# Moving the decoding of float64 weights behind the softplus of the step in front of it, and the split of a gathered tile by one group

## The chip, the cores and the metric

The kernel runs on one core of a Trainium2 chip. The metric is device time in microseconds (us) of one execution; lower is better. Times are of the whole program: attention, a dense softplus layer and a mixture of experts, fused into one launch.

## The reference, cut to what matters

```python
def reference(q, k, v, moe_w_in, moe_w_out, moe2_w_skip, moe2_w_gate, moe2_w1, moe2_w2):
    attn = softmax(rotate(q) @ rotate(k).T / 8) @ v                # 2 x 8 heads x 576 tokens x 64
    x = attn.transpose(0, 2, 1, 3).reshape(1152, 512)
    h = x @ w_in                                                   # 512 x 2048, float64
    x = softplus(h) @ w_out                                        # 2048 x 512, float64
    # softplus: max(h, 0) + log1p(exp(-|h|))
    # then: tokens with x @ w_skip > 0 go to the best of 8 experts (x @ w_gate);
    # out = x + probability * (relu(x @ w1[e]) @ w2[e]); the other tokens keep x
```

The two weight matrices of the middle layer come as float64 and are read by the kernel as 64-bit integers; it turns them into float32 itself.

## The kernel before, in words

Matrix products are made in two parts for accuracy: each operand is split into a rounded high part and the rest (`gh`/`gl`, `xh`/`xl`, two layers of `w`), and three products of the parts are added in PSUM.

The middle layer works in steps. A step (phase, f) takes group f of 128 of the 2048 hidden columns and one chunk of tokens. There are four phases (`ranges`): phase 0 takes tokens 0 to 511 with groups 0 to 5, phase 1 takes tokens 512 to 1151 with all groups 0 to 15, phases 2 and 3 take tokens 0 to 255 and 256 to 511 with groups 6 to 15. In a step, `hidden` issues the products h on TensorE (L581; two halves a and b of 320 tokens in phase 1, one piece of 512 in phase 0), then the softplus: Abs, Relu, Exp, 1+y and Ln on ScalarE (L596, L598, L600, L603, L606), three VectorE instructions (L605, L608, L610), the rounding `gh` on ScalarE (L612) and the rest `gl` on VectorE (L613). `second` multiplies gh and gl with the output weights into acc (L622); it is traced two steps behind `hidden`.

The weights of a group are loaded and decoded once, in `weights`: two halves (w_in and w_out), each of which is one DMA of 512 KB into `raw` (two buffers), three integer instructions on VectorE that put the sign, exponent and mantissa bits together (L563, L564, L565), the rounding on ScalarE (L567) and the rest on VectorE (L568). All decoded groups then stay in SBUF. Groups 0 and 1 are decoded during attention; the table `ahead` says before which step of which phase each other group is decoded: entry (z, fw) of phase p decodes group fw in front of step (p, z).

Each engine works through its own queue in order. Within what the data allow, a scheduler at build time merges the traced instructions into these queues; `issue_after(ins)` makes the instructions of its block that are on the engine of `ins` stand behind `ins` in that queue. It adds no wait between engines.

Near the end of phase 3, `moe2.gather` transposes the first gathered tile of the expert layer and splits it into two parts (L873 on ScalarE and VectorE, named `split`). `XGT` names the step behind which this is traced, and `hidden` of all later steps is put behind `split` by `issue_after`. After the last step a part with a hand-written TensorE order follows: the last groups' products (`rest`), with products mh of the expert layer (L1197) in between.

Of the kernel before, what the change touches and what calls it, by code (L numbers as in the profile page):

```python
# [9 lines left out]
F32 = mybir.dt.float32  # L10
# [31 lines left out]
EARLY = ((2, 11), (3, 9), (3, 10), (3, 11), (3, 12))  # L42

N0 = 6
XGT = (3, 13)
REST = ((12, 13), (14,))


# [487 lines left out]
class Moe1:  # L536
# [34 lines left out]
    def hidden(self, ci, f, hp, tp, gq):  # L571
        nc, w = self.nc, self.w[f]
        c0, n, _ = self.CH[ci]
        nb = 2 if n > 512 else 1
        m = n // nb
        ps = [hp.tile([128, 512], F32, name=f"h{ci}{f}{c}", tag="h") for c in range(nb)]
        z = 0
        for k in range(4):
            for x, src in ((0, self.xh), (0, self.xl), (1, self.xh)):
                for c in range(nb):  # L580
                    nc.tensor.matmul(  # L581
                        ps[c][:, 0:m], lhsT=w[:, 0, x, 128 * k : 128 * k + 128],
                        rhs=src[:, k, c0 + m * c : c0 + m * c + m], start=z == 0, stop=z == 11,
                    )
                z += 1
        def t(nm, dt=F32, bufs=2):
            x = (gq if bufs == 4 else tp).tile([128, 640], dt, name=f"{nm}{ci}{f}", tag=nm, bufs=bufs)
            return x

        y, r, u, gh, gl = t("y"), t("r"), t("u"), t("gh", F32R, 4), t("gl", F32R, 4)  # L590

        ln = u[:, 320 : 320 + n] if n <= 320 else u[:, 0:n]
        y, r, u, gh, gl = (x[:, 0:n] for x in (y, r, u, gh, gl))
        cs = [(ps[c][:, 0:m], slice(m * c, m * c + m)) for c in range(nb)]
        for hv, c in cs:
            nc.scalar.activation(y[:, c], hv, AF.Abs)  # L596
        for hv, c in cs:
            nc.scalar.activation(r[:, c], hv, AF.Relu)  # L598
        for hv, c in cs:
            nc.scalar.activation(y[:, c], y[:, c], AF.Exp, scale=-1.0)  # L600

        for hv, c in cs:
            nc.scalar.activation(u[:, c], y[:, c], AF.Copy, bias=1.0)  # L603
        for hv, c in cs:
            nc.vector.scalar_tensor_tensor(y[:, c], u[:, c], 1.0, y[:, c], op0=ALU.subtract, op1=ALU.subtract)  # L605
            nc.scalar.activation(ln[:, c], u[:, c], AF.Ln)  # L606
        for hv, c in cs:
            nc.vector.tensor_sub(r[:, c], r[:, c], y[:, c])  # L608
        for hv, c in cs:
            nc.vector.tensor_add(r[:, c], r[:, c], ln[:, c])  # L610
        for hv, c in cs:
            nc.scalar.copy(gh[:, c], r[:, c])  # L612
            nc.vector.tensor_sub(gl[:, c], r[:, c], gh[:, c].bitcast(F32))  # L613
        return gh, gl

    def out_mm(self, ci, f, g, acc, f0, f1, only=None):
# [453 lines left out]
def attention_moe_moe_kernel(ctx: ExitStack, tc, q, k, v, w_in, w_out, w_skip, w_gate, w1, w2, tab, out):  # L1070
    nc = tc.nc

    def pool(stack, name, bufs=1, space=None, **kw):
        if space is not None:
            kw["space"] = space
        return stack.enter_context(tc.tile_pool(name=name, bufs=bufs, **kw))
# [10 lines left out]
    with ExitStack() as s1:  # L1087
# [4 lines left out]
        moe1 = Moe1(nc, w_in, w_out, xh, xl)  # L1092
# [25 lines left out]
        with ExitStack() as s2:  # L1118
            gq, gp = pool(s2, "gq"), pool(s2, "gp")
            ring = [(pool(s2, "wb0"), 3), (pool(s2, "wb1"), 2), (wc, 4), (wa, 2)]  # L1120
            tp = pool(s2, "tp")
            hp, accp = pool(s2, "hp", 2, PSUM), pool(s2, "accp", 5, PSUM)
            psa = pool(s2, "psa", 1, PSUM)

            part = tp.tile([128, 4, 512], F32, name="part")
            ranges = ((0, 0, N0), (1, 0, 16), (2, N0, 16), (3, N0, 16))
            steps = [(ph, ci, f) for ph, (ci, f0, f1) in enumerate(ranges) for f in range(f0, f1)]
            due, pend, accs = [], [], {}
            ahead = {0: [(0, 2), (1, 3), (2, 4), (3, 5), (5, 6)],
                     1: [(0, 7), (2, 8), (3, 9), (5, 10), (6, 11), (8, 12), (9, 13), (11, 14), (12, 15)], 2: [], 3: []}  # L1130

            def ready(ph, t):
                if ph == 0:
                    nc.scalar.copy(part[:, t, :], accs[ph][t])
                    return
                x2 = tp.tile([128, 512], F32, name=f"x2{t}", tag="x2", bufs=4)
                if ph == 1:
                    nc.scalar.copy(x2, accs[ph][t])
                else:
                    nc.vector.tensor_add(x2, accs[ph][t], part[:, t, :])  # L1140
                k = 128 * ORDER2.index(t)
                nc.sync.dma_start(x2d[k : k + 128, 0:DM], x2)
                for r, ap in out_rows(out, t):
                    nc.sync.dma_start(ap, x2[r])
                due.append((t, x2))

            def second(group):

                ph, ci = group[0][:2]
                _, f0, f1 = ranges[ph]  # L1150
                ts = Moe1.CH[ci][2]
                if group[0][2] == f0:
                    accs[ph] = {t: accp.tile([128, 512], F32, name=f"acc{ph}{t}", tag="acc") for t in ts}
                last = group[-1][2] == f1 - 1
                for t in ts:
                    for _, _, f, g in group:
                        moe1.out_mm(ci, f, g, accs[ph], f0, f1 - 1, t)
                    if last:
                        ready(ph, t)

            for ph, ci, f in steps:
                for z, fw in ahead[ph]:
                    if z == f:
                        wb, n = ring[(0, 0, 0, 1, 1, 2, 2, 2, 2, 0, 0, 0, 1, 3)[fw - 2]]

                        with ExitStack() as order:
                            for done in att.parted[-2:] if fw >= LATE_W else ():
                                order.enter_context(tc.issue_after(done))
                            moe1.weights(fw, wb, st, n)
                with ExitStack() as order:  # L1170
                    if (ph, f) > XGT:
                        for done in moe2.split:
                            order.enter_context(tc.issue_after(done))
                    pend.append((ph, ci, f, moe1.hidden(ci, f, hp, gp, gq)))
                if len(pend) > 2 and (ph, f) not in HOLD:
                    second([pend.pop(0)])
                if due and (ph, f) >= (2, 10):
                    t, x2 = due.pop(0)
                    moe2.logits(t, moe2.turned(t, x2, hp, tp), psa)
                    if not due:  # L1180
                        moe2.route(*((4, 5) if ph == 2 else (0, 2)), psa)
                if (ph, f) == (2, 15):
                    moe2.first_tile(psa)
                    moe2.fetch(0, sp)
                if (ph, f) in EARLY:
                    c = EARLY.index((ph, f))
                    raw = st.tile([128, 1024], F32, name=f"wr{c}", tag="st", bufs=2)
                    moe2.load_chunk(raw, 0, c)
                    moe2.early.append(moe2.split_w(0, c, raw))
                if (ph, f) == XGT:  # L1190
                    st0 = moe2.gather(0, gq, accp, "acc")
            mh0 = [accp.tile([128, 512], F32, name=f"mh0{c}", tag="acc") for c in range(2)]
            fill = list(moe2.hidden_mm(0, st0, mh0))

            def more(n):
                while n and fill:
                    fill.pop(0)()  # L1197
                    n -= 1

            def rest(t, fs):  # L1200
                for ph, ci, f, g in pend:
                    if f in fs:
                        moe1.out_mm(ci, f, g, accs[ph], N0, 15, t)

            with tc.manual_schedule(engines={nc.tensor.engine}):
                for fs in REST:
                    rest(2, fs)
                    rest(3, fs)
                    more(MORE[4])
                for t in (2, 3):  # L1210
                    rest(t, (15,))
                    ready(3, t)
                more(MORE[0])
                xt = [moe2.turned(t, x2, hp, tp) for t, x2 in due]
                more(MORE[1])
                for (t, _), x in zip(due, xt):
                    moe2.logits(t, x, accp, "acc")
                more(MORE[2])
                moe2.route(2, 2, psa, more)
                more(24)  # L1220
            st0 = moe2.relu(0, st0, sp, mh0)
# [44 lines left out]
```

## Time and profile before

| what | before |
|---|---|
| median of 3 runs | 543.67 us (542.75 to 544.87) |
| the profiled execution | 541.82 us |
| its span of instructions | 540.0 us, so 1.82 us lie around it |
| TensorE (PE) busy | 500.6 us, 93% |
| VectorE (DVE) busy | 437.7 us, 81% |
| ScalarE (ACT) busy | 388.1 us, 72% |
| GpSimd (POOL) busy | 195.8 us, 36%, most of it in attention |
| bytes moved | 67.18 MB, mean 124 GB/s |

Busy shares are means over stages with different limits: attention (about 0 to 210 us), the middle layer (about 183 to 410 us), the experts (about 404 to 540 us). A stage is read by the windows of the trace and by what TensorE waits for in it. PE is the matmul, PEld the load of its stationary operand, which overlaps.

### The profile page before, as it was taken

What the parts mean: (1) busy time and instruction counts of PE and PEld (TensorE: products, weight loads), DVE (VectorE), ACT (ScalarE), POOL (GpSimd) and SP (SyncE); (2) the same over time, 40 slices, a digit from 0 to 9 for tenths busy, and PEclk for the clock granted to TensorE, in tenths of its full rate; (3) what the DMA queues carried; (4) which work ended last, traced back from release to release, by engine and by line L of the source; (5) the groups of instructions that cost most, each with busy time, mean ns of one, the idle gap of its engine ahead of it and who ended that gap; (6) DMA issues with size and microseconds to landing.
All of it is one profiled execution on the core that took longest, in us unless ns stands there. A gap on an engine that the chain in (4) does not pass through costs nothing. (4 is left out here: it accounts for less than half of the span.)

```text
span 540.0 us, 9141 instructions
## 1 busy us (share of the span) xinstructions
PE 500.6 (93%) x2924; PEld 423.8 (78%) x2924; DVE 437.7 (81%) x866; ACT 388.1 (72%) x887; POOL 195.8 (36%) x236
## 2 busy tenths in 40 slices
PE   7899988979988999889999999999998899899994
PEld 3787877857767888779999998999986678677773
DVE  6687876898899999899999944546775789788994
ACT  2588887868877785697676956866783588677881
POOL 2878999979864311000000000001200524522331
PEclk9699999999999999989999999999999999999998
DMA  8797365344354023443433300410325704695300
GB/s 202 189 232 207 81 157 133 100 98 131 94 148 136 2 78 102 139 130 114 142 118 101 134 0 1 157 39 5 126 76 183 286 20 157 215 386 185 117 21 34
DMA packets 43014, 67.18 MB, mean 124 GB/s; under 512 B 9824, under 2 KB 24416, under 8 KB 42960
## 3 DMA queue, kind: packets, MB, share of 16 engines
q1 hardware_dynamic: 39184, 59.60, 37.2%
q0 software_dynamic: 1440, 4.20, 2.1%
q10 hardware_dynamic: 2336, 2.74, 1.6%
q8 instruction: 25, 0.41, 0.3%
q14 instruction: 29, 0.24, 0.2%
HBM read 67.30 MB, written 7.15 MB: 138 GB/s over the span
## 5 line engine op out<-in xcount | busy, mean ns | idle before, releaser
L581 PE MATMUL h<-xh,w 128*128 128x320 f32 (+2 forms) x464 | 105.4, 310 | 0.2 <-ACT P L264 0.2
L622 PE MATMUL acc<-w,gh 128*128 128x512 f32 x288 | 85.0, 401 | 6.1 <-ACT gh L612 6.0
L850 DVE TENSOR_TENSOR ws<-raw,ws 128x1024 fp32r<-128x1024 f32 x67 | 78.8, 1219 | 5.5 <-ACT ws L846 5.3
L581 PEld LDWEIGHTS h<-xh,w 128*128 128x128 f32 x464 | 77.8, 188 | 4.2 <-ACT P L264 0.4
L581 PE MATMUL h<-xl,w 128*128 128x320 f32 (+2 forms) x232 | 69.6, 308 | 0.0
L686 POOL TENSOR_SCALAR sc<-lg 128x2 f32<-128x2 f32 (+1 forms) x3 | 1.0, 327 | 186.5 <-DVE lg L669 186.5
L622 PEld LDWEIGHTS acc<-w,gh 128*128 128x128 f32 x288 | 53.4, 192 | 16.9 <-ACT gh L612 6.8
L846 ACT CAST ws<-raw 128x1024 fp32r<-128x1024 f32 x67 | 66.4, 1062 | 0.2 <-ACT ex L737 0.2
L926 PE MATMUL y<-ws,hT 128*128 128x512 f32 x216 | 57.4, 404 | 1.1 <-DVE ws L850 0.5
L938 POOL DMA_INDIRECT out_dram<-yo,si x9 | 31.5, 3499 | 69.5 <-DVE yo L937 59.2
L264 ACT ACTIVATE P<-s,m 128x576 f32<-128x576 f32 x64 | 48.0, 752 | 10.9 <-DVE m L251 10.5
L251 DVE TENSOR_REDUCE m<-s 128x1 f32<-128x576 f32 x64 | 47.8, 749 | 7.9 <-PE s L243 6.9
L334 PE MATMUL t<-ct,P 128*128 128x128 f32 x288 | 46.2, 283 | 8.1 <-DVE pt L329 3.7
L412 PE MATMUL pv<-pt,vv 128*128 128x320 f32 (+1 forms) x272 | 49.7, 314 | 2.8 <-DVE x L424 2.1
L878 PE MATMUL mh<-ws,xgT 128*128 128x512 f32 x192 | 49.0, 399 | 1.7 <-DVE ws L850 1.3
L622 PE MATMUL acc<-w,gl 128*128 128x512 f32 x144 | 49.3, 392 | 0.0
L596 ACT ACTIVATE y<-h 128x320 f32<-128x320 f32 (+2 forms) x58 | 25.3, 438 | 31.0 <-PE h L581 30.2
L926 PEld LDWEIGHTS y<-ws,hT 128*128 128x128 f32 x216 | 39.0, 188 | 10.8 <-DVE ws L850 1.8
L605 DVE SCALAR_TENSOR_TENSOR y<-u,y 128x320 f32<-128x320 f32 (+2 forms) x58 | 27.3, 484 | 23.0 <-ACT u L603 23.0
L334 PEld LDWEIGHTS t<-ct,P 128*128 128x128 f32 x288 | 34.3, 143 | 14.6 <-DVE pt L329 5.1
L412 PEld LDWEIGHTS pv<-pt,vv 128*128 128x128 f32 x272 | 40.2, 194 | 6.1 <-DVE x L424 3.3
L581 PEld LDWEIGHTS h<-xl,w 128*128 128x128 f32 x232 | 43.3, 188 | 2.1
(266 smaller groups left out, 1122.2 us busy)
## 6 DMA issues: line engine op xcount, KB each, us to landing
raw<-in_moe_w_dram SPq DMA_DIRECT2D x68, 512.0 KB
raw<-in_moe_w_in_dram SPq DMA_DIRECT2D x16, 512.0 KB
raw<-in_moe_w_out_dram SPq DMA_DIRECT2D x16, 512.0 KB
ks<-kT SPq DMA_DIRECT2D x32, 144.0 KB
kl<-kT SPq DMA_DIRECT2D x32, 144.0 KB
qs<-qT SPq DMA_DIRECT2D x32, 128.0 KB
wr<-in_moe_w_dram SPq DMA_DIRECT2D x5, 512.0 KB
x2d<-x SPq DMA_DIRECT2D x9, 256.0 KB
```

The source lines that it names most:

```text
L251: self.latest = nc.vector.tensor_reduce(st["m"][:, a : a + 1], st["ps"][a][:, :, 0:288], axis=AX.XY, op=ALU.max, negate=True)
L264: nc.scalar.activation(P[:, 576 * a : 576 * a + 576].rearrange("p (c n) -> p c n", c=2), ps[:, :, 0:288], AF.Exp, bias=m[:, a : a + 1], ac ...
L334: nc.tensor.transpose(ps[:, 128 * i : 128 * i + 128], src, ident)
L412: nc.tensor.matmul(ps[:, 0:n], lhsT=vv[:, j, :], rhs=pt[:, x, self.place(c, i), 0:n], **se)
L581: nc.tensor.matmul(ps[c][:, 0:m], lhsT=w[:, 0, x, 128 * k : 128 * k + 128], rhs=src[:, k, c0 + m * c : c0 + m * c + m], start=z == 0, stop ...
L605: nc.vector.scalar_tensor_tensor(y[:, c], u[:, c], 1.0, y[:, c], op0=ALU.subtract, op1=ALU.subtract)
L622: nc.tensor.matmul(acc[t], lhsT=g[x][:, 128 * j : 128 * j + 128], rhs=w[:, 1, y, :], start=f == f0 and z == 0, stop=f == f1 and z == 2,)
L846: hi = nc.scalar.copy(w[:, 0], raw)
L850: self.did[T, c] = hi.ins, nc.vector.tensor_sub(w[:, 1], raw, w[:, 0].bitcast(F32)).ins
L878: i = mm()
L926: nc.tensor.matmul(py, lhsT=ht[:, x, o : o + 128], rhs=w[:, y, 512 * j : 512 * j + 512], start=c == 0 and j == 0 and z == 0, stop=c == 3 a ...
L938: nc.gpsimd.indirect_dma_start(out=self.out, out_offset=bass.IndirectOffsetOnAxis(ap=si.bitcast(U32), axis=0), in_=yo, in_offset=None, bou ...
```

## The change

Group 6 is no longer decoded in phase 0; the ten groups 6 to 15 are decoded in phase 1, most of them one step later than before. Their VectorE instructions are put behind `plus`, the last L613 that was traced before them, which is that of the step in front. And `XGT` moves from step (3, 13) to (3, 14).

```diff
-XGT = (3, 13)
+XGT = (3, 14)
...
         for hv, c in cs:
             nc.scalar.copy(gh[:, c], r[:, c])
-            nc.vector.tensor_sub(gl[:, c], r[:, c], gh[:, c].bitcast(F32))
+            self.plus = nc.vector.tensor_sub(gl[:, c], r[:, c], gh[:, c].bitcast(F32))
...
-            ahead = {0: [(0, 2), (1, 3), (2, 4), (3, 5), (5, 6)],
-                     1: [(0, 7), (2, 8), (3, 9), (5, 10), (6, 11), (8, 12), (9, 13), (11, 14), (12, 15)], 2: [], 3: []}
+            ahead = {0: [(0, 2), (1, 3), (2, 4), (3, 5)],
+                     1: [(0, 6), (1, 7), (3, 8), (4, 9), (6, 10), (7, 11), (8, 12), (10, 13), (11, 14), (12, 15)],
+                     2: [], 3: []}
...
                             for done in att.parted[-2:] if fw >= LATE_W else ():
                                 order.enter_context(tc.issue_after(done))
+
+                            if fw >= N0:
+                                order.enter_context(tc.issue_after(moe1.plus.ins))
                             moe1.weights(fw, wb, st, n)
```

No instruction is added or taken away. What the scheduler makes of it is seen at two places.

VectorE where phase 0 ends. Numbers in names are buffers: gl_2983 is of step (0, 4); u_3038 before and u_3021 after are of step (0, 5); u_3108 and u_3091 of step (1, 0); raw_3007 and raw_3015 before, and raw_3047 and raw_3055 after, are the two halves of group 6; raw_3064 is the first half of group 7. Before:

```order
L563 TENSOR_SCALAR wt_3009<-raw_3007 128x512
L564 SCALAR_TENSOR_TENSOR wt_3009<-raw_3007,wt_3009 128x512
L563 TENSOR_SCALAR wt_3017<-raw_3015 128x512
L613 TENSOR_TENSOR gl_2983<-r_2980,gh_2982 128x512
L565 SCALAR_TENSOR_TENSOR wt_3009<-raw_3007,wt_3009 128x512
L564 SCALAR_TENSOR_TENSOR wt_3017<-raw_3015,wt_3017 128x512
L565 SCALAR_TENSOR_TENSOR wt_3017<-raw_3015,wt_3017 128x512
L568 TENSOR_TENSOR w_3006<-wt_3009,w_3006 128x512
L563 TENSOR_SCALAR wt_3066<-raw_3064 128x512
L568 TENSOR_TENSOR w_3006<-wt_3017,w_3006 128x512
L564 SCALAR_TENSOR_TENSOR wt_3066<-raw_3064,wt_3066 128x512
L605 SCALAR_TENSOR_TENSOR y_3036<-u_3038,y_3036 128x512
```

In the change:

```order
L613 TENSOR_TENSOR gl_2983<-r_2980,gh_2982 128x512
L605 SCALAR_TENSOR_TENSOR y_3019<-u_3021,y_3019 128x512
L605 SCALAR_TENSOR_TENSOR y_3089<-u_3091,y_3089 128x320
L608 TENSOR_TENSOR r_3020<-r_3020,y_3019 128x512
L608 TENSOR_TENSOR r_3090<-r_3090,y_3089 128x320
L610 TENSOR_TENSOR r_3020<-r_3020,u_3021 128x512
L610 TENSOR_TENSOR r_3090<-r_3090,u_3091 128x320
L613 TENSOR_TENSOR gl_3023<-r_3020,gh_3022 128x512
L563 TENSOR_SCALAR wt_3049<-raw_3047 128x512
L563 TENSOR_SCALAR wt_3057<-raw_3055 128x512
L605 SCALAR_TENSOR_TENSOR y_3089<-u_3091,y_3089 128x320
```

The softplus of (0, 5) now has no decoding in front of it or in between; group 6 follows it.

VectorE near the end of phase 3. u_5153 is of step (3, 13); u_5196 before and u_5187 after are of (3, 14); u_5230 of (3, 15); xgT is the split. Before:

```order
L613 TENSOR_TENSOR gl_5155<-r_5152,gh_5154 128x256
L873 TENSOR_TENSOR xgT_5178<-xgt_5172,xgT_5177 128x512
L605 SCALAR_TENSOR_TENSOR y_5194<-u_5196,y_5194 128x256
L605 SCALAR_TENSOR_TENSOR y_5228<-u_5230,y_5228 128x256
L608 TENSOR_TENSOR r_5195<-r_5195,y_5194 128x256
L608 TENSOR_TENSOR r_5229<-r_5229,y_5228 128x256
L610 TENSOR_TENSOR r_5195<-r_5195,u_5196 128x256
L610 TENSOR_TENSOR r_5229<-r_5229,u_5230 128x256
L613 TENSOR_TENSOR gl_5198<-r_5195,gh_5197 128x256
L613 TENSOR_TENSOR gl_5232<-r_5229,gh_5231 128x256
```

In the change:

```order
L605 SCALAR_TENSOR_TENSOR y_5185<-u_5187,y_5185 128x256
L608 TENSOR_TENSOR r_5152<-r_5152,y_5151 128x256
L608 TENSOR_TENSOR r_5186<-r_5186,y_5185 128x256
L610 TENSOR_TENSOR r_5152<-r_5152,u_5153 128x256
L610 TENSOR_TENSOR r_5186<-r_5186,u_5187 128x256
L613 TENSOR_TENSOR gl_5155<-r_5152,gh_5154 128x256
L613 TENSOR_TENSOR gl_5189<-r_5186,gh_5188 128x256
L873 TENSOR_TENSOR xgT_5212<-xgt_5206,xgT_5211 128x512
L605 SCALAR_TENSOR_TENSOR y_5228<-u_5230,y_5228 128x256
L608 TENSOR_TENSOR r_5229<-r_5229,y_5228 128x256
```

Step (3, 14) has moved from behind the split to in front of it, beside (3, 13); ScalarE's order moves in the same way.

## Rows read from the trace of the kernel before

**Rows 1.** The page, part 1: busy us (share of the span) and instructions of each engine.

```profile
PE 500.6 (93%) x2924; PEld 423.8 (78%) x2924; DVE 437.7 (81%) x866; ACT 388.1 (72%) x887; POOL 195.8 (36%) x236
```

**Rows 2.** Waits of PE from 190 to 425 us: total, times, longest.

```profile
PE acc L622 <- ACT gh L612: 6.0, 2, 4.0
```

**Rows 3.** Windows: length; busy us of PE, PEld, DVE, ACT, POOL; granted clock; DMA share; GB/s.

```profile
227.20:231.20 4.00, 0.00 (x0) 0.00 (x0) 4.00 (x9) 3.31 (x9) 0.00 (x0) 1.00 0.42 133
231.20:240.00 8.80, 8.79 (x40) 7.72 (x41) 8.80 (x20) 7.59 (x19) 0.00 (x0) 0.81 0.25 80
250.00:260.00 10.00, 10.00 (x62) 9.39 (x61) 9.85 (x23) 5.94 (x16) 0.00 (x0) 1.00 0.41 116
400.00:410.00 10.00, 8.02 (x41) 6.49 (x40) 5.78 (x15) 4.67 (x15) 0.00 (x0) 1.00 0.42 159
```

**Rows 4.** Timeline of PE, phase 0 to 1: start us, length, instructions, [idle before].

```profile
208.90 1.98 PE L622 MATMUL acc<-w,gh 128*128 128x512 f32 x8
...
226.74 0.31 PE L581 MATMUL h<-xl,w 128*128 128x320 f32 x1
226.89 0.31 PE L581 MATMUL h<-xh,w 128*128 128x320 f32 x1
231.21 4.14 PE L622 MATMUL acc<-w,gh 128*128 128x512 f32 x10 [4.02 <-ACT gh L612]
235.19 1.09 PE L622 MATMUL acc<-w,gl 128*128 128x512 f32 x4
```

**Rows 5.** Timeline of DVE, the same place.

```profile
224.15 0.43 DVE L563 TENSOR_SCALAR wt<-raw 128x512 uint32<-128x512 uint32 x1 [1.42 <-DMA raw<-in_moe_w_in_dram]
...
225.70 1.09 DVE L605 SCALAR_TENSOR_TENSOR y<-u,y 128x512 f32<-128x512 f32 x2
226.87 0.43 DVE L563 TENSOR_SCALAR wt<-raw 128x512 uint32<-128x512 uint32 x1
227.21 0.69 DVE L565 SCALAR_TENSOR_TENSOR wt<-raw,wt 128x512 uint32<-128x512 uint32 x1
...
228.82 0.48 DVE L608 TENSOR_TENSOR r<-r,y 128x320 f32<-128x320 f32 x1
229.22 0.68 DVE L564 SCALAR_TENSOR_TENSOR wt<-raw,wt 128x512 uint32<-128x512 uint32 x1
229.82 0.69 DVE L610 TENSOR_TENSOR r<-r,u 128x512 f32<-128x512 f32 x1
```

**Rows 6.** Timeline of ACT, the same place.

```profile
222.25 0.64 ACT L567 CAST w<-wt 128x512 fp32r<-128x512 f32 x1
222.76 1.02 ACT L603 ACTIVATE u<-y 128x512 f32<-128x512 f32 x2
...
226.42 0.99 ACT L606 ACTIVATE u<-u 128x512 f32<-128x512 f32 x2 [1.07 <-DVE y L605]
...
230.54 0.62 ACT L612 CAST gh<-r 128x512 fp32r<-128x512 f32 x1
...
235.63 2.05 ACT L1134 COPY part<-acc 128x512 f32<-128x512 f32 x4 [0.30 <-PE acc L622]
```

**Rows 7.** Timeline of PE and ACT near the end of phase 3.

```profile
398.38 0.28 PE L581 MATMUL h<-xh,w 128*128 128x256 f32 x1
...
404.13 0.61 PE L1197 MATMUL mh<-ws,xgT 128*128 128x512 f32 x2
406.73 0.73 PE L622 MATMUL acc<-w,gh 128*128 128x512 f32 x2 [1.98 <-ACT gh L612]
...
401.83 0.58 ACT L873 CAST xgT<-xgt 128x512 fp32r<-128x512 f32 x1
...
406.27 0.74 ACT L612 CAST gh<-r 128x256 fp32r<-128x256 f32 x2 [0.92 <-DVE r L610]
```

**Rows 8.** Timeline of SP's queue, one issue, and of DVE, its use.

```profile
258.31 0.33 SPq L557 DMA_DIRECT2D raw<-in_moe_w_out_dram  x1
...
262.87 0.43 DVE L563 TENSOR_SCALAR wt<-raw 128x512 uint32<-128x512 uint32 x1 [0.51 <-DMA raw<-in_moe_w_out_dram]
```

## The prediction

> **What bounds the kernel.** The page comes first: TensorE is busy for 93% of the span, VectorE for 81% [rows 1]. These are means over three stages, and the change touches only the middle one, so next come TensorE's waits from 190 to 425 us. There are two of any size, 4.0 and 2.0 us, and both are a product into acc that waits for ScalarE's rounding gh [rows 2]. In between TensorE issues without a gap that the trace shows. So the middle layer is bound by TensorE, and the change can gain what these two stalls cost; it can lose by making new ones.
>
> The windows then tell what happens in the first stall [rows 3]. From 227.2 to 231.2 TensorE does nothing while VectorE is busy for 4.00 of 4.00 us: the softplus that gh belongs to stands in a full queue. The window behind these 4 idle microseconds has a granted clock of 0.81, a mean of the levels 2.4 GHz (1.00) and 1.2 GHz (0.50); it is 1.00 in the row of 250 to 260, where VectorE is still busy for 9.85 of 10 us. The last row holds the second stall: TensorE 8.02 of 10.
>
> The timelines say whose softplus. TensorE's last product of h of step (1, 0) starts at 226.89 [rows 4]; with 0.15 us from one 320-wide start to the next it is free at 227.04. What it wants next is gh of (0, 5), and that comes at 231.21. On VectorE the decoding of groups 6 and 7 stands in front of this softplus and within it [rows 5]: a first L563 that waited 1.42 us for its DMA, then L605 only at 225.70, and L563, L565 and L564 before L610 at 229.82. On ScalarE two L567 of group 6 stand in front of L603, each 0.51 (222.25 to 222.76), and gh is issued at 230.54 [rows 6].
>
> **First stall: −5.7.** The change takes group 6 out of phase 0, and the decoding behind gl of (0, 5). Without its two L567, L603 of (0, 5) starts 2 × 0.51 = 1.02 earlier, at 221.74, and has its first result some 0.6 later, about 222.4 (0.64 is the length of a cast of this shape). L605 then starts at 222.45 in place of 225.70. From L605 to gh it took 230.54 − 225.70 = 4.84; L563, L565 and L564 in between have pitches of 0.34, 0.60 and 0.60 (226.87 to 227.21, 229.22 to 229.82), so 1.54 goes and 3.30 stays: gh starts at 225.75, ends 0.62 later at 226.37. TensorE asks at 227.04. The stall of 4.02 goes with 0.6 to spare.
>
> With it goes the slow stretch behind it. The ten gh products behind the stall last 4.14, at a time when the clock is 0.81 [rows 3, 4]. At full clock eight last 1.98 and four gl 1.09, so one costs (1.98 − 1.09)/4 = 0.2225, and ten would last 1.09 + 6 × 0.2225 = 2.43. That is 1.71 lost; 0.19 × 8.8 us = 1.67 says the same. Which of the two levels a stretch gets is not proved by rows at one stall alone, so the bounds of this part are 4.0 and 5.7; I take 5.7, since TensorE is idle nowhere else near.
>
> Next late would be gh of (1, 0), half b: in front of it on ScalarE stand four copies of the finished accumulators, 2.05 us [rows 6]. Its place in the queue makes it ready about 0.3 us before TensorE, now earlier, asks. If I am wrong there, up to 1 us comes back; that widens the range and nothing else.
>
> **Second stall: −2.0.** The last h of (3, 14) is done on TensorE at 398.38 + 0.28 = 398.66, but its softplus stands behind ScalarE's split at 401.83, and both last gh come at 406.27, for which TensorE waits 1.98 until 406.73 [rows 7]. In the change (3, 14) runs beside (3, 13), in front of the split. From the end of the split (402.41) to gh it took 3.86, for a pair of steps; begun at 398.66 with (3, 13) as its partner the same chain gives 402.5, and I add 0.3 for what stands between: 402.8. TensorE asks for it at 406.73 − 1.98 = 404.75. The split then runs from about 403.1 to 403.7, and mh wants its first part at 404.13. What is late next is gh of (3, 15), alone behind the split: the pair's 3.86, less the partner's Abs and Relu (four of these took 1.07, so 0.5) and the partner's place in three VectorE instructions (0.3 each), is 2.5, so about 406.2. TensorE, unstalled, has six products of (3, 14) and two mh first, 8 × 0.22 = 1.8, and asks at 406.5. The bounds are 0 and 2.0; I take 2.0, with only 0.3 to spare.
>
> **Phase 1: 0, if VectorE keeps up.** Nothing is added, but group 6 and most others now fall into phase 1 or later in it. One group costs VectorE 2 × (0.34 + 3 × 0.60) = 4.28, with 0.60 taken for L568 too (the same shape), and one step's softplus in two halves eight instructions of 0.40 (228.82 to 229.22), 3.2 [rows 5]. From step 3 to step 12 that is 8 × 4.28 + 10 × 3.2 = 66.2. TensorE takes 24 × 0.15 + 15 × 0.2225 = 6.94 a step, 69.4 for the ten. That leaves 3.2 for waits. The waits come from the two raw buffers: the next load can start only when L565 has read the last, and the L563 of the next group now stands with everything behind it in VectorE's queue. From issue to use such a load takes 262.87 − 258.31 = 4.56, and 0.51 of that was already waited for [rows 8]. Where two decodings are one step apart (five times among these), 3.2 of softplus and about 0.7 of L568 lie in between, 3.9, so 0.66 is waited each time: 3.3. VectorE and TensorE come out level, 69.5 against 69.4. Softplus of a step is asked for two steps later, and I count about 4 us of slack in it and in the weights (group 15 is ready about 3.6 before its use; it was 23). So I cost this at nothing: the cover is that slack, and without it each further microsecond of VectorE's costs one. Bounds 0 and +3: none to all of the waits in the open. SP's queue holds the same loads in the same order, each behind the buffer that it fills; no other work stands behind them for long. ScalarE has room (5.94 of 10 busy). Phases 2 and 3 lose no instruction and gain none, and nothing else in them moves against its neighbours: they start earlier as they are.
>
> **Sum.** −5.7 − 2.0 = −7.7. The profiled execution took 541.82, so 534.1 in its place. The median of before is 543.67, 1.85 above it; on that footing the forecast is **536.0**.
>
> **The rivals.**
> *Only one stall goes.* If the second is replaced by a wait for gh of (3, 15) or for the split (0.3 to spare, [rows 7]), 543.7 − 5.7 = 538.0. If instead the first comes back at the boundary of the phases, where two L563 now wait for loads with the softplus of (1, 0) behind them, only the second goes: 541.7. For the latter speaks that VectorE stays full; against it that gh of (0, 5) now stands in front of all decoding.
>
> *VectorE becomes the bound (the slower side).* Its place is the pair of L563 at the head of each decoding in phase 1. It waits for both loads, softplus of the next step stands behind it, gh behind that, TensorE behind gh. VectorE is level with TensorE already, so the price is all extra waiting over the slack of 4. To end 0.5% above before, the five close decodings must wait (4 + 7.7 + 2.7)/5 = 2.9 more each, that is a load of 7.5 rather than 4.6; at 3.2 more, 16 − 4 = 12 is lost, and 536 + 12 = 548. Against it: the DMA engines are busy for 0.41 of 250 to 260 [rows 3], so a load has no reason to slow down.
>
> *The gain is larger.* TensorE's even pitch says it is full. Its weight loads are busy for 9.39 of 10 us there, which leaves 0.6 in ten; over 165 us of middle layer that is 10 us that could hide small waits for operands. If the new order removed them too, about 526. Against it, the pitch does not vary as waits would. The Trainium skill ("Perfetto Trace Analysis", "Identifying the Most-Contended Engine") holds that matmul busy time is a poor measure of headroom and the busy share of the weight loads a good one. By that rule the stretch is 94% full and not 100%; the sum by it would be the 526 above.
>
> *It does nothing,* because the order of the engines that matter comes out as before: 543.7. The rows of order speak against that at both places.
>
> **Chances.** Forecast 0.62, its own range 534 to 538.5. Second stall replaced 0.13 (538.0). Only the second goes 0.10 (541.7). VectorE the bound 0.08 (548). Larger gain 0.03 (526). Nothing 0.04 (543.7). The range from 533.5 to 541.7 holds the first three, 0.85, with the larger gain, VectorE as the bound and no effect outside. A measurement of this kernel can tell about 0.5%, 2.7 us, from no change: below 541.0 is faster, above 546.4 slower. Faster: 0.62 + 0.13 + 0.03 and a third of the third (where the stall comes back, but not the slow clock behind it), 0.81; slower 0.08; the same 0.11.
>
> **What would show it.** Right: among TensorE's waits no 4 us for gh near 227, granted clock 1.00 from 227 to 240, everything behind some 5.7 earlier; no 2 us wait near 399 in front of the last products; VectorE's waits for raw in phase 1 at most 0.7 each. Wrong: TensorE waits for gh, or for a w that L568 makes, between 230 and 325; or the rest near 397 waits for gh of (3, 15).

## The result and the profile after

| | median us | runs | ratio to before, 95% interval |
|---|---|---|---|
| before | 543.21 | 542.25 to 544.87 (4) | |
| changed | 536.63 | 533.77 to 537.26 (4) | 0.986 (0.982 to 0.990) |
| changed, nothing edited (e10) | 537.44 | 536.52 to 537.89 (4) | 0.9866 (0.9843 to 0.9890) |

The change gains 6.6 us by the medians, where the sum forecast 7.7 and 536.0; again 6.7 in the last row, which was measured later, beside runs of before with a median of 544.13. The ratio is not the quotient of the two medians (0.988); its interval holds both that and the forecast (536.0/543.67 = 0.986). The profiled execution of the changed kernel took 536.4 us with a span of 534.6, against 541.82 and 540.0.

TensorE's waits from 195 to 420 us, all of them (what was waited for; total, times, longest). They answer to [rows 2]:

```profile
PE ht L909 <- ACT hs L898: 0.5, 1, 0.5
PE y L926 <- DVE hT L912: 0.2, 1, 0.2
PE y L926 <- ACT hT L911: 0.2, 1, 0.2
PE acc L622 <- DVE pt L329: 0.2, 1, 0.2
```

Both waits for gh are gone. The windows, beside [rows 3]:

```profile
227.20:231.20 4.00, 4.00 (x22) 3.47 (x21) 3.66 (x8) 4.00 (x12) 0.00 (x0) 1.00 0.01 2
231.20:240.00 8.80, 8.80 (x49) 7.88 (x48) 8.39 (x20) 7.82 (x20) 0.00 (x0) 1.00 0.35 122
240.00:400.00 160.00, 160.00 (x991) 145.66 (x990) 127.85 (x315) 119.73 (x316) 4.19 (x9) 1.00 0.29 95
406.90:410.30 3.40, 3.40 (x10) 2.34 (x9) 1.51 (x9) 1.63 (x3) 0.80 (x4) 0.53 0.13 42
```

TensorE is busy throughout 227 to 231, and the granted clock is 1.00 in these windows up to 400. The last row is new: for 3.4 us behind the middle layer the clock falls to 0.53, near its lower level.

TensorE's timeline, beside [rows 4, 7]:

```profile
184.00 0.50 PE L581 MATMUL h<-xh,w 128*128 128x512 f32 x1 [0.17 <-ACT P L264]
...
228.13 2.45 PE L622 MATMUL acc<-w,gh 128*128 128x512 f32 x10
230.42 1.07 PE L622 MATMUL acc<-w,gl 128*128 128x512 f32 x4
...
321.24 0.30 PE L581 MATMUL h<-xh,w 128*128 128x320 f32 x1
...
321.82 0.75 PE L581 MATMUL h<-xh,w 128*128 128x320 f32 x4
...
391.03 0.18 PE L711 MATMUL rk<-extra,cb 1*128 1x16 bf16 x1
...
399.38 0.63 PE L1201 MATMUL mh<-ws,xgT 128*128 128x512 f32 x2
399.85 0.62 PE L622 MATMUL acc<-w,gh 128*128 128x512 f32 x2
...
401.22 0.61 PE L1201 MATMUL mh<-ws,xgT 128*128 128x512 f32 x2
401.91 0.73 PE L622 MATMUL acc<-w,gh 128*128 128x512 f32 x2
...
403.86 1.14 PE L656 MATMUL x2t<-ct,x 128*128 128x128 f32 x8
405.13 1.95 PE L666 MATMUL lgp<-w,x2T 128*128 128x9 f32 x16
406.94 3.60 PE L1201 MATMUL mh<-ws,xgT 128*128 128x512 f32 x8
410.34 0.44 PE L711 MATMUL rk<-oh,cb 128*128 128x16 bf16 x9
```

The same places in before, as far as they are not among the rows above:

```profile
182.91 0.50 PE L581 MATMUL h<-xh,w 128*128 128x512 f32 x1 [0.17 <-ACT P L264]
...
395.79 0.18 PE L711 MATMUL rk<-extra,cb 1*128 1x16 bf16 x1
...
410.48 1.15 PE L656 MATMUL x2t<-ct,x 128*128 128x128 f32 x8
...
413.56 2.09 PE L1197 MATMUL mh<-ws,xgT 128*128 128x512 f32 x8
415.50 0.38 PE L711 MATMUL rk<-oh,cb 128*128 128x16 bf16 x9
```

The ten gh last 2.45, not 4.14, and follow the last h without a gap. At 399.85 gh of (3, 14) follows mh at once; before, 1.98 lay between. At 401.91 gh of (3, 15) comes 0.69 behind the start of the mh pair, where two products take 0.46: a new wait of 0.23, which the list of waits does not show. The eight mh at 406.94 last 3.60; in before the same eight took 2.09.

ScalarE's timeline, beside [rows 6, 7]:

```profile
222.82 1.01 ACT L603 ACTIVATE u<-y 128x512 f32<-128x512 f32 x2
...
226.90 0.61 ACT L612 CAST gh<-r 128x512 fp32r<-128x512 f32 x1
...
397.42 0.74 ACT L612 CAST gh<-r 128x256 fp32r<-128x256 f32 x2 [0.92 <-DVE r L610]
398.07 0.58 ACT L873 CAST xgT<-xgt 128x512 fp32r<-128x512 f32 x1
...
401.45 0.41 ACT L612 CAST gh<-r 128x256 fp32r<-128x256 f32 x1 [1.03 <-DVE r L610]
```

VectorE's timeline: the softplus of (0, 5), and then the last decoding of phase 1, beside [rows 5, 8]:

```profile
223.50 1.09 DVE L605 SCALAR_TENSOR_TENSOR y<-u,y 128x512 f32<-128x512 f32 x2 [3.75 <-ACT u L603]
...
304.58 0.43 DVE L563 TENSOR_SCALAR wt<-raw 128x512 uint32<-128x512 uint32 x1 [1.25 <-DMA raw<-in_moe_w_in_dram]
...
314.60 0.43 DVE L563 TENSOR_SCALAR wt<-raw 128x512 uint32<-128x512 uint32 x1 [0.80 <-DMA raw<-in_moe_w_out_dram]
...
319.77 0.68 DVE L568 TENSOR_TENSOR w<-wt,w 128x512 fp32r<-128x512 f32 x1
```

VectorE now waits for (0, 5)'s Exp chain instead of standing in decoding. Its waits for loads from 228 to 330 us (total, times, longest):

```profile
DVE wt L563 <- DMA raw<-in_moe_w_out_dram: 3.1, 5, 0.8
DVE wt L563 <- DMA raw<-in_moe_w_in_dram: 1.3, 1, 1.3
```

**Where the time went.** The timelines of TensorE of the two kernels are cut at the same instructions. "Middle" runs from the h behind gl of (0, 4) (221.76 before, 222.85 after) to the last rank product (rk) of phase 3 (395.79, 391.03); x2t are the eight transposes behind the last product of the middle layer:

| stretch | before | after | difference | forecast |
|---|---|---|---|---|
| attention, up to the first h | 182.91 | 184.00 | +1.09 | 0 |
| middle, up to the first gl of (0, 5) | 13.43 | 7.57 | -5.86 | -5.73 |
| middle, from there on | 160.60 | 160.61 | 0.0 | 0 |
| first mh to last x2t row (second stall) | 6.35 | 4.48 | -1.87 | -1.98 |
| last x2t to the next rank product | 5.02 | 6.48 | +1.46 | 0 |
| experts, from there to the end | 124.50 | 124.26 | -0.24 | 0 |

The sum is -5.4, the difference of the spans. The two stretches that are left out took the same in both: 38.85 us in front of the middle, and 8.34 and 8.35 between the last rank product of phase 3 and the first mh.

### The profile page after: what moved, and what is told of

The parts are those of the page before. It is cut to its first block, busy times and chain, and to the rows that moved or that the text cites. A ratio compares the mean times of both kernels' runs of the same rounds, so it can differ in the third digit from the quotient of the medians.

```text
span 534.6 us, 9132 instructions
## 1 busy us (share of the span) xinstructions
PE 499.3 (93%) x2924; PEld 422.3 (79%) x2924; DVE 437.1 (82%) x866; ACT 387.0 (72%) x887; POOL 195.2 (37%) x236
## 5 line engine op out<-in xcount | busy, mean ns | idle before, releaser
L850 DVE TENSOR_TENSOR ws<-raw,ws 128x1024 fp32r<-128x1024 f32 x67 | 79.0, 1217 | 4.9 <-ACT ws L846 4.7
L622 PE MATMUL acc<-w,gh 128*128 128x512 f32 x288 | 81.2, 395 | 0.2 <-DVE pt L329 0.2
L622 PEld LDWEIGHTS acc<-w,gh 128*128 128x128 f32 x288 | 52.1, 188 | 10.2 <-ACT gh L612 0.6
L622 PE MATMUL acc<-w,gl 128*128 128x512 f32 x144 | 47.6, 393 | 0.0
L878 PEld LDWEIGHTS mh<-ws,xgT 128*128 128x128 f32 x192 | 35.0, 188 | 11.7 <-DVE ws L850 4.1
```

Source lines behind the costliest of these rows:

```text
L622: nc.tensor.matmul(acc[t], lhsT=g[x][:, 128 * j : 128 * j + 128], rhs=w[:, 1, y, :], start=f == f0 and z == 0, stop=f == f1 and z == 2,)
L850: self.did[T, c] = hi.ins, nc.vector.tensor_sub(w[:, 1], raw, w[:, 0].bitcast(F32)).ins
L878: i = mm()
```

## Experiments

The first four take the change apart.

**e1: the table alone.**

```diff
-            ahead = {0: [(0, 2), (1, 3), (2, 4), (3, 5), (5, 6)],
-                     1: [(0, 7), (2, 8), (3, 9), (5, 10), (6, 11), (8, 12), (9, 13), (11, 14), (12, 15)], 2: [], 3: []}
+            ahead = {0: [(0, 2), (1, 3), (2, 4), (3, 5)],
+                     1: [(0, 6), (1, 7), (3, 8), (4, 9), (6, 10), (7, 11), (8, 12), (10, 13), (11, 14), (12, 15)],
+                     2: [], 3: []}
```

> The new table alone (group 6 as the first entry of phase 1, no order behind gl, split after (3, 13)). Theory: what removes the first stall is VectorE's order, not the table; here L605 of (0, 5) still stands behind group 6 and half of group 7, word for word as before, so TensorE waits 4.0 us for gh of (0, 5), the clock falls behind it, and the median is that of before (ratio 0.998 to 1.002). Rival: taking group 6 out of phase 0 is what counts; then the stall goes here too and the time falls by 5.7 (ratio 0.9895).

Measured: 543.53 us, ratio 0.9995 (0.9978 to 1.0013). The first line of TensorE's list of waits (total, times, longest):

```profile
PE acc L622 <- ACT gh L612: 6.2, 2, 4.2
```

The table alone changes nothing: the order of instructions on all five engines comes out the same as before, row for row. Tracing the decoding a step later does not hold it back; I take this to be because the scheduler puts ready decoding into VectorE's queue wherever it finds room. So this run also shows what no change measures as.

**e2: the order behind gl alone,** with the old table and the old `XGT`.

```diff
+            self.plus = nc.vector.tensor_sub(gl[:, c], r[:, c], gh[:, c].bitcast(F32))
...
+                            if fw >= N0:
+                                order.enter_context(tc.issue_after(moe1.plus.ins))
```

> The order behind gl alone, with the table of before (group 6 still in phase 0, behind gl of (0, 4); split after (3, 13)). Theory: L605 of (0, 5) comes at about 222.95 instead of 225.70, since only seven instructions of group 6 and none of group 7 stand in front of it; gh of (0, 5) is then ready at about 227.5 and TensorE asks at 227.04, so a stall of 0.5 us stays and some 5 us are gained (ratio 0.991). Rival (the table counts): no gain, ratio 1.0.

Measured: 536.16 us, ratio 0.9858 (0.9827 to 0.9890), as much as the whole change. TensorE's wait for gh that is left, and the ten gh in its timeline:

```profile
PE acc L622 <- ACT gh L612: 2.0, 1, 2.0
```

```profile
228.60 0.31 PE L581 MATMUL h<-xh,w 128*128 128x320 f32 x1
229.04 2.56 PE L622 MATMUL acc<-w,gh 128*128 128x512 f32 x10
```

TensorE is free 0.15 after the start of the last h, so the wait is 229.04 - 228.75 = 0.29 where 0.5 was expected. The middle takes 168.62 (before 174.03): 5.4 gained by the order alone, 0.45 less than the change gains there. Behind the second stall the clock falls (first mh to last x2t 7.97, before 6.35), which gives 1.6 back. That leaves 3.8 of the 7.3 us measured; 2.8 more come from the expert stage (121.66, before 124.50), which the edit doesn't touch (see e9). The remaining 0.7 are not accounted for: the stretches are those of one profiled execution, 7.3 is a difference of medians.

**e3: table and order, split where it was.** Against the changed kernel:

```diff
-XGT = (3, 14)
+XGT = (3, 13)
```

> Table and order, split after (3, 13) as before. Theory: the first stall and its slow clock go (5.9 us), the second stall of 2.0 us stays: ratio 0.989, 537.6 where before is 543.5. Of the clock behind the middle layer: if TensorE's fall to 0.53 at 407 in the changed kernel comes from having no stall in front of it, it stays at 1.00 here.

Measured: 539.25 us, ratio 0.9912 (0.9883 to 0.9942). The middle takes 168.17 as in the changed kernel, the second stall of 2.0 is there as in before, but the clock now falls behind it: from the first mh to the last x2t it takes 7.97 where before took 6.35. That is 1.62 of the 5.86 given back, and 4.2 was measured. The window of the slow stretch, just behind the stall:

```profile
403.30:406.70 3.40, 3.40 (x10) 2.68 (x9) 0.33 (x1) 0.00 (x0) 0.00 (x0) 0.50 0.33 120
```

My guess that the clock falls only where no stall precedes is wrong.

**e4: the split alone.** Against before:

```diff
-XGT = (3, 13)
+XGT = (3, 14)
```

> The split after (3, 14) alone, decoding as before. Theory: only the second stall goes, 2.0 us (ratio 0.9965); if the granted clock then falls for 3.4 us behind it as in the changed kernel, 1.5 of it is given back and the ratio is 0.999. Rival: the terms depend on each other, and without the earlier start of phase 1 the second stall stays: 1.0.

Measured: 540.45 us, ratio 0.9942 (0.9921 to 0.9963). The second stall goes by itself (first mh to last x2t 4.50), so the two terms do not depend on each other. The clock falls behind it (x2t to rank 6.15, 1.1 given back), and the experts take 122.16, 2.3 less than in before: that is more than the split's own gain.

**e8: is the slow clock due to the idle time?** Before, with products nobody uses in the first stall. The new products stand behind `lasth`, the last h that was traced, and gh of (0, 5) stands behind the last of them; a VectorE copy of 8 of their columns comes with them.

```diff
+                if (ph, group[0][2]) == (0, 5):
+                    d = psa.tile([128, 512], F32, name="fed", tag="ra")
+                    order.enter_context(tc.issue_after(moe1.lasth.ins))
+                    for i in range(18):
+                        fd = nc.tensor.matmul(
+                            d, lhsT=moe1.w[0][:, 0, 0, 0:128], rhs=moe1.w[0][:, 1, 0, :], start=i == 0, stop=i == 17)
...
+                            if (ph, group[0][2]) == (0, 5):
+                                o2.enter_context(tc.issue_after(fd.ins))
+                            moe1.out_mm(ci, f, g, accs[ph], f0, f1 - 1, t)
```

> Before, with 18 more products (512 columns, 4.0 us at 0.2225) that nothing uses, on TensorE between the last h in front of the first stall and gh of (0, 5), so that TensorE is busy instead of idle there. Theory: the slow clock behind the stall is due to the idle time. The granted clock then stays at 1.00 from 227 to 240, ten gh last 2.43 us instead of 4.14, and the middle layer takes 1.7 us less (174.0 becomes 172.3) though more is computed. Rival: the fall of the clock has nothing to do with the idle time, and the ten gh are as slow as before (174.0). In both cases the total may move by what the scheduler does to the expert stage.

Measured: 542.81 us, ratio 0.9998 (0.9980 to 1.0016). Its windows, TensorE's timeline and ScalarE's gh of (0, 5):

```profile
228.70:232.80 4.10, 4.10 (x20) 3.22 (x19) 4.10 (x9) 3.35 (x9) 0.00 (x0) 1.00 0.40 130
232.80:240.00 7.20, 7.20 (x41) 6.49 (x41) 7.17 (x17) 6.69 (x17) 0.00 (x0) 1.00 0.25 75
```

```profile
228.70 4.27 PE L1160 MATMUL fed<-w 128*128 128x512 f32 x18
232.80 2.57 PE L622 MATMUL acc<-w,gh 128*128 128x512 f32 x10
...
232.10 0.62 ACT L612 CAST gh<-r 128x512 fp32r<-128x512 f32 x1
```

The clock stays at 1.00 and the ten gh last 2.57 instead of 4.14, with gh as late as before (232.10, less the 1.53 by which attention ended later, is 230.57; before 230.54). This is one profile, but the mean granted clock of whole executions says the same: 0.983 over ten of e8, 0.980 over the twenty of before beside them, and 0.003 of 540 us is 1.6 us. So the idle 4 us cost their own length and some 1.6 more through the clock, and the slow stretch belonged to the first term. The middle takes 172.94, 1.1 less rather than 1.7: 160.60 behind the first gl became 161.15, since the scheduler ordered this stretch anew.

**e6 and e7: how much cover VectorE has in phase 1.** The changed kernel with L564 repeated, which leaves its result as it is (e7 without `and i == 0`):

```diff
             nc.vector.scalar_tensor_tensor(tu, hi, 0xC0000000, tu, op0=ALU.bitwise_and, op1=ALU.bitwise_or)
+            if f >= N0 and i == 0:
+                nc.vector.scalar_tensor_tensor(tu, hi, 0xC0000000, tu, op0=ALU.bitwise_and, op1=ALU.bitwise_or)
```

> The changed kernel with one more L564 (0.60 us of VectorE, same result) for one half of each of the groups 6 to 15, 6.0 us in all, to measure the cover of VectorE in phase 1. Theory after the trace of the changed kernel: L568 of group 15 starts 0.8 us before the first h that needs it has passed, and VectorE was idle for some 5 us in phase 1, 2 of it behind ScalarE: 2 to 5 us longer in the middle layer (168.2 becomes 170 to 173), with TensorE waiting for w of L568 or for gh. Rival, the prediction's cover of 4 us: 0 to 1 us.

> The same with one more L564 in both halves, 12.0 us in all. Theory: everything above the cover is paid in full, 8 to 11 us more in the middle layer (176 to 179). Rival, cover of 4 us in front of group 15 and 4.8 us of it used by steps before 3: 5 to 7 us more. If VectorE is not the bound at all: under 2.

Measured: e6 541.50 us, 0.9962 (0.9948 to 0.9977); e7 544.00 us, 1.0007 (0.9991 to 1.0023). The middle takes 171.48 and 175.99, against 168.18. So 3.3 of 6.0 and 7.8 of 12.0 us are paid, and 2.7 and 4.2 are covered; e6 lies within what I expected, e7 just under it, and the 0 to 1 us of e6's rival is wrong. 3.3 is half of what the change gains, 7.8 is all of it. What TensorE waits for, e6 and then e7 (their lines stand two lower: L583 is h, L569 and L570 are the two parts of w):

```profile
PE h L583 <- ACT w L569: 2.2, 1, 2.2
PE acc L624 <- ACT gh L614: 0.3, 1, 0.3
```

```profile
PE h L583 <- DVE w L570: 2.9, 3, 1.1
PE h L583 <- ACT w L569: 1.7, 3, 1.0
PE acc L624 <- ACT gh L614: 0.3, 1, 0.3
PE acc L624 <- DVE gl L615: 0.3, 1, 0.3
```

The listed waits make 2.5 of the 3.3 us and 5.2 of the 7.8. It is the weights that come late first, not the softplus as my rival had it.

**e5: old table, order, new split.** The changed kernel with the table of before:

```diff
-            ahead = {0: [(0, 2), (1, 3), (2, 4), (3, 5)],
+            ahead = {0: [(0, 2), (1, 3), (2, 4), (3, 5), (5, 6)],
...
```

> The table of before (group 6 still in phase 0), the order behind gl, and the split after (3, 14). Theory: from the first h of phase 1's second step to the rank product at the end of phase 3 it takes 168.6 us as with the order alone (changed kernel 168.2, before 174.0), and the second stall goes as in the changed kernel (1.9). What the expert stage takes is not derived: the scheduler orders it anew in every version (124.3 to 124.5 us behind the last rank product in before and in the changed kernel, 121.7 and 122.2 with the order alone and the split alone). If it is of the short kind, about 533 us in all; of the long kind, 536.

Measured: 536.51 us, ratio 0.9874 (0.9855 to 0.9894). Middle 168.63, first mh to last x2t 4.49, experts 124.57, the long kind, and no fall of the clock between them. That is the time of the changed kernel, without its table: what the table adds to the order is the 0.45 us of the middle, too little to be seen in the times.

**e9 and e11: why the experts take 122 or 124.5.** The first row is from VectorE's waits in before behind 415 us, the second from those of e2:

```profile
DVE si L935 <- DMA out_dram<-yo,si: 5.1, 2, 3.0
```

```profile
DVE si L935 <- DMA out_dram<-yo,si: 1.0, 1, 1.0
```

si is a column of 128 row numbers, with three buffers; a fourth must wait until the scatter (the DMA that writes finished rows to the output) that reads the first is done. In the long kind L935 stands early in VectorE's queue, with L850 behind it. So, on the changed kernel (e9) and on e5 (e11):

```diff
-        si = xp.tile([128, 1], I32, name=f"si{T}", tag="si", bufs=3)
+        si = xp.tile([128, 1], I32, name=f"si{T}", tag="si", bufs=9)
```

> The changed kernel with nine buffers for si (L934) in place of three. In the expert stage of before, of the changed kernel and of the two versions with 124.3 to 124.6 us behind the last rank product, VectorE's L935 waits 4.9 to 5.1 us in two waits for the DMA that reads an earlier si, with L850 and so TensorE behind it; in the two versions with 121.7 and 122.2 it waits 1.0. Theory: these waits are the difference, so the stage falls from 124.3 to about 122 and the total by 2.3 us (534 where the changed kernel is 536.5). Rival: the yo buffer (L937) is read by the same DMA and waits in its place; no gain.

> The same nine buffers on the version with the table of before, the order behind gl and the split after (3, 14). Theory: the same, 2.3 us less than that version (534); with the middle layer at 168.6 it is level with the changed kernel and nine buffers. Rival: L937 waits instead, 536.5.

Measured, beside e10 on the same chip (537.44): e9 535.74 us, 0.9846 (0.9823 to 0.9870); e11 535.27 us, 0.9831 (0.9806 to 0.9857). The experts take 122.95 and 122.58. In e9 the wait for the scatter is gone; a smaller one, for the gathered rows, is left:

```profile
DVE yo L937 <- PE y L926: 1.8, 1, 1.8
DVE si L935 <- DMA xg<-x2d,gi: 1.5, 2, 1.1
```

In the profiles 1.3 and 2.0 of the 2.3 expected are gained, and yo did not wait in its place: its 1.8 for y is there in before too. Both beat before clearly; against the changed kernel the medians are 1.7 and 2.2 lower, with intervals that overlap. Part of that can be the clock, which does not fall behind the middle layer in the profiles of e9 and e11 and does in that of e10. So the wait for the scatter is shown to go, and that it makes the whole difference between 122 and 124.5 is not shown.

**e10: the changed kernel again.**

> The changed kernel once more, nothing edited, for a ratio from more executions and a second profile. Theory: the middle layer takes 168.2 us again and both stalls are gone, since these follow from the order; whether the granted clock falls for some 3.4 us behind the last products of the middle layer (1.5 us, in the first profile yes) and when attention ends (184.0; 182.9 in the profile of before, 184.5 to 186.5 in the others) differ from execution to execution. Ratio 0.987. Rival: the fall of the clock there belongs to the program, then it is there again.

Measured: the ratio in the first table. The middle takes 168.17 (168.18), first mh to last x2t 4.48 (4.48): the two terms repeat to 0.01 us. The fall of the clock came again, later and longer (0.57 over 408 to 414), and reached into the experts, which took 126.0 where the first profile of the same kernel has 124.3. So I cannot say that it is chance; e5, e9 and e11 have the same hand-written TensorE order there and no fall.

## Why the prediction was right

**First stall: right, and step by step.** Less the 1.09 us by which attention ended later, the changed kernel has L603 at 221.73 (forecast 221.74), L605 at 222.41 (222.45), gh at 225.81 (225.75) and TensorE free at 227.04 (227.04): 0.6 to spare, as said. The term was 5.73 and is 5.86. e8 shows that its second half, the slow clock, hung on the idle time. One name was wrong: the last h in front of the stall belongs to step (1, 1), second half, and not to (1, 0); its times are what I used, so no number changes.

**Second stall: right, but what I had to spare was mis-sized.** Taking off 4.76, by which TensorE runs earlier there, gh of (3, 14) was forecast for 398.04 and came at about 397.75 (it is the second of the pair at 397.42); gh of (3, 15) for 401.44 and came at 401.45. I had 0.3 in hand for the latter, but I set the start of gh against the moment at which TensorE asks, and left out the 0.41 that the rounding itself takes (in the first stall I had counted it). With it 0.1 was missing by my own figures; 0.23 was missing in the run, since TensorE is free at about 401.68 and gh is done at 401.86. So 1.87 is gained of 1.98: that the slip cost so little is luck. e4 shows that the stall goes by the split alone.

**Phase 1: the cost was 0, as taken, but the size of the slack was wrong in one place.** "Group 15 is ready about 3.6 before its use" is off: its first half ends at 319.77 + 0.68 = 320.45, h of (1, 15) starts at 321.24, and the fifth of its products, the first that reads what this L568 makes, at 321.82: 0.8 to 1.4. I had counted 0.66 for five waits for loads. In the trace L563 waits for loads in six places up to 1.25, 4.4 us together, not 3.3; so one sign that I had named, waits for raw of at most 0.7 each, did not hold, and the time held all the same. The cover, 2.7 us by e6 and 4.2 by e7, is at most about the 4 I gave it. What runs out first are the weights, and the rival "VectorE becomes the bound" named the wrong thing behind it: not the softplus behind the pair of L563, but h that waits for w. Its price is borne out: by the prediction 4 + 7.7 = 11.7 us more on VectorE bring back the time of before, and e7, with 12.0 more, has a ratio of 1.0007. No run made the loads slower, which was the rival's condition, so its chance of 0.08 was not tested.

**The larger gain did not come.** The middle from the first gl of (0, 5) on takes 160.60 before and 160.61 after, with another order of VectorE and ScalarE. I take it that TensorE was full there. The Trainium skill ("Perfetto Trace Analysis", "Identifying the Most-Contended Engine") judges headroom by the busy share of the weight loads, together with the share of peak arithmetic that is reached. Here the first of these is 145.66 of 160, 91%, in a stretch that no version made shorter, so in these versions the even start-to-start times were the better sign.

**What the sum left out, and what hid it.** Three parts outside it moved: attention (+1.09), the clock behind the middle layer (+1.46) and the experts (-0.24). Attention ended at 182.91 in the profile of before and between 184.0 and 186.5 in all twelve others, e1 with its unchanged order among them: the profiled execution of before was a lucky one (e1's ended 1.54 later, and its whole span is 1.6 longer), which is the greater part of its 1.85 below the median. Working on the medians was right for that reason. That the clock would fall behind the middle layer was not foreseen. It costs 1.46 in the profile, and would explain why the medians show 6.6 and 6.7 where the sum has 7.7; the intervals are too wide to show it. That the scheduler orders the expert stage anew with every edit in the middle layer was missed too. That it cost nothing here was luck: it is worth 2.3 to 2.8 us in e2 and e4, and without the cut into stretches e2 would have read as "the order alone does all of it, the split nothing".

## What to carry to other kernels

Where the busiest engine stalls once at a change of phase, walk that one chain back through the queues: the sum of what stands in front of it gave the stall and the slow clock behind it to 0.13 us. Compare the end of what is waited for, not its start, with the moment at which it is asked for. Moving where something is traced may move nothing; read the order that comes out, and pin it behind a named instruction if it matters. When a scheduler orders the whole program, compare versions stretch by stretch at the same instructions, since an edit here may cost or give microseconds in a stage that it never touched.

## What was unexpected of the hardware

In and behind the middle layer TensorE's granted clock fell to its lower level, 1.2 GHz, for some 3.4 us (6.8 in e10), in eight of the thirteen profiles at one place, in e4 at two, and in e5, e8, e9 and e11 at none. The places are behind the first stall (before, e1, e4), behind the second stall (e2, e3), and behind the sixteen products of 128x9 that follow the middle layer, with no listed wait in front (changed kernel, e4, e6, e7, e10). The falls whose cost can be read off cost 1.1 to 1.7 us, the longer one of e10 more. With the first stall filled (e8) the clock fell at none of these places, although e8 has the second stall; and before has the second stall and the small products without a fall there. So idle time brings the first one; what decides the others was not settled.
